# A float64 weight conversion rewritten in 128x512 pieces on VectorE and ScalarE, and the scores and softmax sums of an attention kernel rescheduled

## The chip, the cores and the metric

One core of one Trainium2 chip runs the whole kernel. The metric is device time in microseconds (us) of one execution. Engines are called by the profile's names: PE (TensorE matmul; PEld is its weight load), DVE (VectorE), ACT (ScalarE), POOL (GpSimd) and SP (SyncE, which here only issues DMAs).

## The reference

Attention over 8 batches, 8 heads, 576 positions and a head size of 64, with a threshold under the softmax, feeds a two-layer network with a quick GELU. The two weight matrices arrive as float64, everything else as float32.

```python
scores = scale * np.matmul(q, k.transpose(0, 1, 3, 2))
thresh = np.max(scores, axis=-1, keepdims=True) - tau
scores = np.where(scores >= thresh, scores, -1000000000.0)
scores = scores - np.max(scores, axis=-1, keepdims=True)
attn = np.exp(scores)
attn = attn / (np.sum(attn, axis=-1, keepdims=True) + 1e-09)
out = np.matmul(attn, v)
...
h = x @ w_in                       # x: 4608 x 512, w_in: 512 x 2048
g = h * (1.0 / (1.0 + np.exp(-1.702 * h)))
return (g @ w_out).astype(np.float32)   # w_out: 2048 x 512
```

## The kernel before, in words

**Attention.** The 64 heads are taken as 32 pairs, four to a batch. For a pair, DVE transposes q and k in 32x32 blocks (`prep`, L282), and PE makes the scores with the keys on the partitions: four main tiles of 128 keys and one tail tile that holds the last 64 keys of both heads. `scores` (L291 to L310) makes four matmuls for a main tile (two heads by two halves of the queries) into two PSUM tiles of the pool `psA`, which has three; each `ps` tile is copied to SBUF by ACT (`keep`, L328, 128x576). DVE takes maxima over groups of 32 keys (`in_groups`, L342), finishes them in a few small steps (`over_tiles`, `over_groups`, `lower`: L348 to L371), spreads the thresholds over the keys (`spread_max`, L376) and subtracts them (`sub`, L384 and L387). ACT drives what lies below the threshold far down (`mask`, a Prelu of a steep slope, L393) and takes the exponential (`exps`, L397). PE multiplies by the values (`values`, tile `pv`, L411). The sums of the exponentials come from PE for pairs 0 to 7 (`sums_by_pe`, tile `den`, also L411: matmuls with ones) and from pair 8 on from DVE (`in_groups` once more, with add; the constant is `BY_PE`). DVE turns the sums round and scales the result into the network's input `xT` (`spread_sums`, `place_x`: L459 to L478).

**The network.** The 4608 rows are nine blocks of 512. For each block PE makes 16 groups of four matmuls (`mm1`, tile `hps`, L490), ACT a tanh (L498), DVE the product `gT` (L501), and then PE four groups of 16 matmuls (`mm2`, tile `ops`, L509). One program matmul of float32 shows as two records in the trace. Block 0 needs pairs 0 to 3; block 1 holds rows of batches 0 and 1, so its first matmul needs `xT` of pairs 4 to 7.

**The weights.** `pieces` are 64 parts of 128x256: first w_in, then w_out. Each is loaded twice, once as it lies (`w64`) and once shifted by three bytes (`w64s`), so that exponent and 28 bits of mantissa can be cut out as 32-bit integers. `cv_open` on DVE makes mantissa `frac` (L239, L243) and exponent `ex` (L248); `cv_mant` on ACT (L256) makes the mantissa a float; `cv_exp` and `cv_end` on POOL (L262, L265, L272) clamp and shift the exponent and multiply. Three pieces can be in load and two in conversion.

**The order.** A planner at the end of the kernel writes each engine's instructions in a fixed order: every step is a `task` with an engine, an assumed cost, a rank, the tasks it follows, and the buffers it takes and gives (`limits`). `run_in_order` plays these through and, on each free engine, starts the ready task of lowest rank. mm1 and mm2 have the highest rank number, so PE takes them only where no attention step is ready. On the chip each engine then works through its list in order and waits at semaphores. While block 0 has not begun, the pairs 1 and 3 use the space of `gT` for their buffers (`APART`).

Of the kernel before, what the change touches and what calls it, by code (L numbers as in the profile page):

```python
# [10 lines left out]
FP32 = mybir.dt.float32  # L11
# [8 lines left out]
P = 128  # L20
GELU_SCALE = 1.702
EPS = 1e-9
BIG = 3.0e38
# [7 lines left out]
def kernel(  # L31
# [62 lines left out]
    neg = const.tile([P, 1], FP32, name="neg")  # L94
    scl = const.tile([P, 1], FP32, name="scl")
    gap = const.tile([P, 1], FP32, name="gap")
# [8 lines left out]
              "raw0": 1, "raw1": 1, "qkT0": 1, "qkT1": 1, "v_m": 2, "w64": 3, "cv": 2}  # L105
# [57 lines left out]


# [44 lines left out]
    WC = 256  # L209
    wide = moe_w_in.dtype != FP32  # L210
    pieces = [(w_in, moe_w_in, c, j) for j in range(d_ff // WC) for c in range(NDC)]
    pieces += [(w_out, moe_w_out, c, j) for c in range(NFC) for j in range(d_model // WC)]
    cv = {}

    def load_w(i):
# [7 lines left out]
        t = work.tile([P, WC, 2], U32, name="w64", tag="w64", bufs=3)  # L223
        nc.sync.dma_start(out=t.rearrange("p c w -> p (c w)"), in_=dram.bitcast(U32))
        t3 = work.tile([P, WC, 2], U32, name="w64s", tag="w64s", bufs=3)
# [4 lines left out]
        cv[i] = [t, t3]  # L230


    def cv_open(i):
        t, t3 = cv[i]
        hi = t[:, :, 1]


        frac = work.tile([P, WC], I32, name="frac", tag="frac")
        nc.vector.tensor_scalar(  # L239
            out=frac, in0=t3[:, :, 0].bitcast(I32), scalar1=0x0FFFFFFF, scalar2=0x10000000,  # L240
            op0=ALU.bitwise_and, op1=ALU.bitwise_or,
        )
        nc.vector.scalar_tensor_tensor(  # L243
            out=frac, in0=hi.bitcast(I32), scalar=31, in1=frac,
            op0=ALU.arith_shift_right, op1=ALU.bitwise_xor,
        )
        ex = work.tile([P, WC], U32, name="ex", tag="ex")
        nc.vector.tensor_scalar(  # L248
            out=ex, in0=hi, scalar1=20, scalar2=0x7FF,
            op0=ALU.logical_shift_right, op1=ALU.bitwise_and,  # L250
        )
        cv[i] = [frac, ex]

    def cv_mant(i):
        mant = work.tile([P, WC], FP32, name="mant", tag="mant")
        nc.scalar.activation(out=mant, in_=cv[i][0], func=AF.Copy, scale=2.0**-28)  # L256
        cv[i][0] = mant

    def cv_exp(i):

        ex = cv[i][1]
        nc.gpsimd.tensor_scalar(  # L262
            out=ex, in0=ex, scalar1=1150.0, scalar2=896.0, op0=ALU.min, op1=ALU.max
        )
        nc.gpsimd.tensor_scalar(  # L265
            out=ex, in0=ex, scalar1=-896.0, scalar2=2.0**23, op0=ALU.add, op1=ALU.mult
        )

    def cv_end(i):
        dst, _, c, j = pieces[i]  # L270
        mant, ex = cv.pop(i)
        nc.gpsimd.tensor_tensor(  # L272
            out=dst[:, c, ts(j, WC)], in0=mant, in1=ex.bitcast(FP32), op=ALU.mult
        )
# [19 lines left out]
    def scores(n, t):  # L294
        qT, kT = mats[n, 0], mats[n, 1]
        if t == NKT:
            ps = [psA.tile([P, 2, 512], FP32, name="ps", tag="ps")]
            for c in range(2):
                nc.tensor.matmul(  # L299
                    ps[0][:, c, 0:SH], lhsT=kd[n % 2], rhs=qT[:, ts(c, SH)],  # L300
# [3 lines left out]
        else:  # L304
            ps = [psA.tile([P, 2, 512], FP32, name="ps", tag="ps") for _ in range(2)]
            for c in range(2):
                for h in range(2):
                    nc.tensor.matmul(  # L308
                        ps[h][:, c, 0:SH],
                        lhsT=kT[ts(h, D), ts(t, P)], rhs=qT[ts(h, D), ts(c, SH)],  # L310
                        start=True, stop=True,
                    )
        pss[n, t] = ps

    def keep(n, t, h):
        ps = pss[n, t][h]
        if t == NKT:
            st = work.tile([P, S], FP32, name="s_t", tag="s_t", bufs=2)
            o = st
        else:  # L320
            if h == 0:
# [400 lines left out]
```

## Time and profile before

| what | value |
|---|---|
| median of three timed runs (lowest, highest) | 1480.32 us (1479.87, 1480.63) |
| the profiled execution: time, span in the profile | 1479.97 us, 1478.2 us |
| PE, DVE, ACT, POOL busy | 1417.4, 988.5, 662.2, 113.2 us |
| PE's instructions: `ops` and `hps` (network) | 1152 + 1152 records |

In the profile, a row of a timeline has start, length (both us), engine, line, operation, tiles, shape and count, and in brackets the idle time before it with what ended it. "busy" counts overlapping instructions of an engine once; the mean of a group counts each instruction in full. The chain of waits lists pieces of the chain that ended last as start, length, what, and a record count that holds matmuls and weight loads or halves of matmuls as they came.

### The profile page before, as it was taken

Reading aid. Unit: us, or ns where it says so; the run is one execution under the profiler, and the core shown is the slowest. Engines: PE = TensorE matmul, PEld = TensorE weight load, DVE = VectorE, ACT = ScalarE, POOL = GpSimd, SP = SyncE. Lnnn points to the kernel's source line nnn. Section 1 sums busy time; section 2 is a strip of 40 time slices with the busy share of each in tenths; the row PEclk is TensorE's granted clock in tenths of the full one; section 3 lists DMA queues with packets and bytes.
Section 4 is the critical chain, followed back from the end, with each engine's and each line's share of the span. In section 5 each row is a group of like instructions: output and inputs, shape, how many; then the busy total and the mean of one; then the engine's idle time right before and its main releaser. Section 6 shows DMA issues by size and latency. Waiting matters only on the chain.

```text
span 1478.2 us, 14382 instructions
## 1 busy us (share of the span) xinstructions
PE 1417.4 (96%) x5056; PEld 661.5 (45%) x5056; DVE 988.5 (67%) x1678; ACT 662.2 (45%) x917; POOL 113.2 (8%) x204
## 2 busy tenths in 40 slices
PE   6888948999999999999999999999999999999998
PEld 3443414444444444444444444444444444444443
DVE  7989898448888888878788887888767840200200
ACT  6774443445544554555455555565444530100100
POOL 0127675000000000000000000000000000000000
PEclk9999979999999999999999999999999999999999
DMA  7236865210111111111111111111111000000000
GB/s 132 67 91 211 236 216 159 40 38 18 25 36 43 32 25 32 39 32 24 25 39 39 24 24 32 39 32 24 32 39 24 1 8 22 0 7 22 0 7 22
DMA packets 214296, 72.23 MB, mean 49 GB/s; under 512 B 193232, under 2 KB 201424, under 8 KB 214224
## 3 DMA queue, kind: packets, MB, share of 16 engines
q1 hardware_dynamic: 211856, 71.02, 19.7%
q8 instruction: 40, 0.66, 0.2%
q10 hardware_dynamic: 2368, 0.30, 0.2%
q14 instruction: 32, 0.26, 0.1%
HBM read 61.84 MB, written 9.44 MB: 48 GB/s over the span
## 4 chain that ended last, share of the span: by engine, by line
PE 82%; DVE 11%; DMA 2%; issue 2%; ACT 2%; SPq 0%; DVEq 0%; ACTq 0%
PE ops L509 31%; PE hps L490 30%; PE pv L411 9%; PE ps L308 8%; PE ps L299 2%; DVE frac L239 1%; DVE ex L248 1%; PE den L411 1%; DVE part L342 1%; DMA w64s<-in_moe_w_out_dram 1%; DVE s_m L384 1%; DVE frac L243 1%; DVE gT L501 1%; DVE s_t L387 0%; DVE qkT L282 0%
## 5 line engine op out<-in xcount | busy, mean ns | idle before, releaser
L509 PE MATMUL ops<-w_out,gT 128*128 128x512 f32 x1152 | 513.8, 600 | 22.4 <-POOL w_out L272 21.3
L490 PE MATMUL hps<-xT,w_in 128*128 128x512 f32 x1152 | 509.6, 596 | 4.9 <-DVE gT L501 4.2
L342 DVE TRANSPOSE_TENSOR_REDUCE part<-s_m 128x36 f32<-128x1152 f32 x216 | 290.3, 1361 | 111.7 <-ACT s_m L328 107.2
L509 PEld LDWEIGHTS ops<-w_out,gT 128*128 128x128 f32 x1152 | 215.8, 191 | 294.4 <-issue 259.5
L490 PEld LDWEIGHTS hps<-xT,w_in 128*128 128x128 f32 x1152 | 215.0, 190 | 273.8 <-issue 249.2
L328 ACT COPY s_m<-ps 128x576 f32<-128x576 f32 x240 | 142.0, 641 | 251.6 <-PE ps L308 251.4
L501 DVE SCALAR_TENSOR_TENSOR gT<-th,hps 128x512 f32<-128x512 f32 x144 | 96.7, 672 | 213.4 <-ACT th L498 212.8
L393 ACT ACTIVATE s_m<-s_m 128x1152 f32<-128x1152 f32 x120 | 138.3, 1153 | 71.6 <-DVE s_m L384 71.5
L498 ACT ACTIVATE th<-hps 128x512 f32<-128x512 f32 x144 | 84.9, 590 | 185.1 <-PE hps L490 185.1
L308 PE MATMUL ps<-qkT 64*128 64x288 f32 x960 | 154.3, 436 | 12.5 <-DVE qkT L282 10.0
L397 ACT ACTIVATE s_m<-s_m,shift,scl 128x1152 f32<-128x1152 f32 x120 | 161.3, 1344 | 2.8
L384 DVE TENSOR_TENSOR s_m<-s_m,mb 128x1152 f32<-128x1152 f32 x120 | 156.7, 1352 | 0.8
L308 PEld LDWEIGHTS ps<-qkT 64*128 64x128 f32 x960 | 86.5, 189 | 106.2 <-ACT s_m L328 37.7
L411 PE MATMUL pv<-s_m,v_m 128*64 128x288 f32 x960 | 125.7, 414 | 0.0
L516 ACT ACTIVATE osb<-ops 128x512 f32<-128x512 f32 x36 | 21.3, 592 | 211.4 <-PE ops L509 211.4
L411 PEld LDWEIGHTS pv<-s_m,v_m 128*64 128x64 f32 x960 | 67.7, 139 | 61.6 <-issue 7.6
L256 ACT ACTIVATE mant<-frac 128x256 f32<-128x256 int32 x64 | 26.2, 415 | 55.2 <-DVE frac L243 55.0
L282 DVE STREAM_TRANSPOSE qkT<-q_raw 128x576 f32<-128x576 f32 x30 | 23.3, 776 | 40.1 <-PE ps L299 36.7
L387 DVE TENSOR_TENSOR s_t<-s_t,mb 64x576 f32<-64x576 f32 x60 | 45.1, 752 | 0.4
L342 DVE TRANSPOSE_TENSOR_REDUCE part_t<-s_t 128x18 f32<-128x576 f32 x56 | 41.8, 747 | 1.4 <-ACT s_t L397 0.4
L376 DVE STREAM_TRANSPOSE mb<-thr 128x1152 f32<-128x1152 f32 x30 | 41.3, 1377 | 0.9
L262 POOL TENSOR_SCALAR ex<-ex 128x256 uint32<-128x256 uint32 x64 | 30.6, 477 | 120.9 <-DVE ex L248 119.4
(64 smaller groups left out, 754.1 us busy)
## 6 DMA issues: line engine op xcount, KB each, us to landing
out_dram<-osb SPq DMA_DIRECT2D x36, 256.0 KB, 2.0
q_raw<-in_q_dram SPq DMA_DIRECT2D x120, 72.0 KB, 2.4
k_raw<-in_k_dram SPq DMA_DIRECT2D x116, 72.0 KB, 2.4
v_m<-in_v_dram SPq DMA_DIRECT2D x64, 128.0 KB, 2.4
w<-in_moe_w_in_dram SPq DMA_DIRECT2D x32, 256.0 KB, 3.1
w<-in_moe_w_out_dram SPq DMA_DIRECT2D x32, 256.0 KB, 3.4
w64s<-in_moe_w_in_dram SPq DMA_DIRECT2D x32, 255.6 KB, 3.4
w64s<-in_moe_w_out_dram SPq DMA_DIRECT2D x32, 255.6 KB, 3.7
```

The source lines that it names most:

```text
L308: nc.tensor.matmul(ps[h][:, c, 0:SH], lhsT=kT[ts(h, D), ts(t, P)], rhs=qT[ts(h, D), ts(c, SH)], start=True, stop=True,)
L328: nc.scalar.copy(out=halves(o), in_=ps[:, :, 0:SH])
L342: nc.vector.tensor_reduce(out=o, in_=i, axis=AXL.X, op=op, apply_transpose=True)
L384: nc.vector.tensor_tensor(out=s, in0=s, in1=mb, op=ALU.subtract)
L387: nc.vector.tensor_tensor(out=s[ts(h, D)], in0=s[ts(h, D)], in1=mb[ts(h, D), h, :], op=ALU.subtract)
L393: nc.scalar.activation(out=s, in_=s, func=AF.Prelu, alpha=STEEP)
L397: nc.scalar.activation(out=s, in_=s, func=AF.Exp, scale=scl, bias=shift)
L411: nc.tensor.matmul(o[c][ts(h, D), 0:SH], lhsT=lhsT, rhs=rhs, start=(t == 0), stop=(t == NKT),)
L490: nc.tensor.matmul(hidden[j], lhsT=w_in[:, c, ts(j, P)], rhs=xTs[blk][:, c, :], start=(c == 0), stop=(c == NDC - 1),)
L498: nc.scalar.activation(out=ths[j], in_=hidden[j], func=AF.Tanh, scale=GELU_SCALE / 2)
L501: nc.vector.scalar_tensor_tensor(out=gT[j], in0=ths.pop(j), scalar=1.0, in1=hidden.pop(j), op0=ALU.add, op1=ALU.mult)
L509: nc.tensor.matmul(acc[i], lhsT=gT[j][:, ts(i, P)], rhs=w_out[:, j, :], start=(j == 0), stop=(j == NFC - 1),)
```

## The change

It does six things.

- Weight pieces are 128x512 (32 instead of 64). All steps work in place, in the loaded words. DVE cuts out the exponent (`cv_ex`, L258 of the changed kernel), ACT turns it into a power of two with one Relu (`cv_power`, L266), DVE cuts out the mantissa (`cv_frac`, L272 and L276), and one DVE instruction converts, scales and multiplies (`cv_end`, L284). POOL has no part any more, and there is no clamp from above.
- Loads land in one of two `w64`/`w64s` buffer pairs or in one of four parts of `w_out` itself (`stage`), of four rows each. A piece of `w_out` may be written only when the stage that lies over it is through.
- The ranks move: w_in pieces have ranks from 3.6 to 4.1, w_out pieces from 3.84 to 4.74 (before: 3.2 to 4.2 for both).
- `scores` makes one `ps` tile from two matmuls, one for each head, for one half of the queries; it is a task of its own, so a main tile has two such tasks, each with one `ps` buffer and one `keep`.
- `BY_PE` is 5: sums of pairs 5, 6 and 7 come from DVE.
- The scale of the scores moves from the exponential to the subtraction, which becomes a scalar_tensor_tensor (L394, L400); the exponential keeps only the pointer `shift`.

```diff
-    WC = 256
+    WC = 512
...
+    STAGES = 4
+    PER_STAGE = NFC // STAGES
+
+    def stage(i):
+
+        if i < n_in:
+            return i % (STAGES + 2) if i % (STAGES + 2) < STAGES else None
+        i -= n_in
+        return STAGES - 1 if i % 3 == 0 and i < NFC - PER_STAGE else None
...
+        x = stage(i)
+        if x is None:
+            t = work.tile([P, WC, 2], U32, name="w64", tag="w64", bufs=2)
+            t3 = work.tile([P, WC, 2], U32, name="w64s", tag="w64s", bufs=2)
+        else:
+            rows = [w_out[:, ds(PER_STAGE * x + 2 * y, 2), :] for y in range(2)]
...
+    def cv_ex(i):
+        hi, ex, _ = cv[i]
         nc.vector.tensor_scalar(
             out=ex, in0=hi, scalar1=20, scalar2=0x7FF,
             op0=ALU.logical_shift_right, op1=ALU.bitwise_and,
         )
...
+    def cv_power(i):
+
+        ex = cv[i][1].bitcast(I32)
+        nc.scalar.activation(out=ex, in_=ex, func=AF.Relu, scale=2.0**23, bias=rebias)
...
+    def cv_frac(i):
+
+
+        hi, _, frac = cv[i]
+        nc.vector.tensor_scalar(
+            out=frac.bitcast(I32), in0=frac.bitcast(I32), scalar1=0x0FFFFFFF,
+            scalar2=0x10000000, op0=ALU.bitwise_and, op1=ALU.bitwise_or,
+        )
+        nc.vector.scalar_tensor_tensor(
+            out=frac.bitcast(I32), in0=hi.bitcast(I32), scalar=31, in1=frac.bitcast(I32),
+            op0=ALU.arith_shift_right, op1=ALU.bitwise_xor,
         )
 
     def cv_end(i):
         dst, _, c, j = pieces[i]
-        mant, ex = cv.pop(i)
-        nc.gpsimd.tensor_tensor(
-            out=dst[:, c, ts(j, WC)], in0=mant, in1=ex.bitcast(FP32), op=ALU.mult
+        _, power, frac = cv.pop(i)
+        nc.vector.scalar_tensor_tensor(
+            out=dst[:, c, ts(j, WC)], in0=frac.bitcast(I32), scalar=2.0**-28,
+            in1=power.bitcast(FP32), op0=ALU.mult, op1=ALU.mult,
         )
...
+        ps = psA.tile([P, 2, 512], FP32, name="ps", tag="ps")
...
+            for h in range(2):
+                nc.tensor.matmul(
+                    ps[:, h, 0:SH],
+                    lhsT=kT[ts(h, D), ts(t, P)], rhs=qT[ts(h, D), ts(c, SH)],
+                    start=True, stop=True,
+                )
...
-            nc.vector.tensor_tensor(out=s, in0=s, in1=mb, op=ALU.subtract)
+            nc.vector.scalar_tensor_tensor(
+                out=s, in0=s, scalar=scl, in1=mb, op0=ALU.mult, op1=ALU.subtract
+            )
...
-        nc.scalar.activation(out=s, in_=s, func=AF.Exp, scale=scl, bias=shift)
+        nc.scalar.activation(out=s, in_=s, func=AF.Exp, bias=shift)
...
-    BY_PE = 8
+    BY_PE = 5
...
-        a = task("SP", 1.1, rank, load_w, i, take=("w64",), lag=3.5)
-        a = task("DVE", 1.0, rank, cv_open, i, after=[a], take=("cv",), give=("w64",))
-        m = task("ACT", 0.42, rank, cv_mant, i, after=[a])
-        e = task("POOL", 1.0, rank, cv_exp, i, after=[a])
-        ready_w.append(task("POOL", 0.9, rank, cv_end, i, after=[e, m], give=("cv",)))
+        x = stage(i)
+        place = ("w64",) if x is None else (f"stage{x}",)
+        a = task("SP", 1.1, rank, load_w, i, take=place, lag=5.0)
+        e = task("DVE", 0.44, rank, cv_ex, i, after=[a])
+        m = task("ACT", 0.72, rank, cv_power, i, after=[e])
+        a = task("DVE", 1.14, rank, cv_frac, i, after=[e])
+
+        over = [ready_w[y] for y in range(i) if i >= n_in and stage(y) == (i - n_in) // PER_STAGE]
+        ready_w.append(task("DVE", 0.72, rank, cv_end, i, after=[a, m] + over, give=place))
```

On DVE, this is what stands before, in the middle of block 0's first half (`gT<-th,hps` is the network's product, `frac`, `ex` and `w` the conversion, a number behind a name its buffer):

```order
L501 SCALAR_TENSOR_TENSOR gT<-th,hps 128x512
L239 TENSOR_SCALAR frac<-w64s 128x256
L243 SCALAR_TENSOR_TENSOR frac<-w_944,frac 128x256
L248 TENSOR_SCALAR ex<-w_944 128x256
L348 TENSOR_REDUCE red<-part 128x36
```

And this is what stands there now, a little later in the program, among the pieces of w_out:

```order
L272 TENSOR_SCALAR w64s<-w64s 128x512
L276 SCALAR_TENSOR_TENSOR w64s<-w_1236,w64s 128x512
L515 SCALAR_TENSOR_TENSOR gT<-th,hps 128x512
L284 SCALAR_TENSOR_TENSOR w_out<-w64s,w_1236 128x512
L258 TENSOR_SCALAR w_1253<-w_1253 128x512
```

A piece costs DVE four instructions of twice the length instead of three, for twice the elements; the product into `w_out` has come over from POOL. Up to the last step of pair 3 on DVE, 8 pieces of 256 were opened before; now 10 pieces of 512 are opened and 7 of them finished. The last `cv_end` now stands inside pair 5's subtractions; before, the last `cv_open` stood behind pair 5's `place_x`.

On PE, before, a late pair's scores stand in four groups with two network matmuls between them (`pv` the values of the pair before, `ps` scores, `kd` the tail tile):

```order
L411 MATMUL pv<-s_t,v_t_74 64x288 x4
L308 MATMUL ps<-qkT 128x288 x4
L490 MATMUL hps<-xT,w_in 128x512 x2
L308 MATMUL ps<-qkT 128x288 x4
L490 MATMUL hps<-xT,w_in 128x512 x2
L308 MATMUL ps<-qkT 128x288 x4
L490 MATMUL hps<-xT,w_in 128x512 x2
L308 MATMUL ps<-qkT 128x288 x4
L299 MATMUL ps<-qkT,kd_73 128x288 x2
L490 MATMUL hps<-xT,w_in 128x512 x24
```

Now the same place reads:

```order
L425 MATMUL pv<-s_t,v_t_74 64x288 x4
L504 MATMUL hps<-xT,w_in 128x512 x6
L319 MATMUL ps<-qkT 128x288 x16
L312 MATMUL ps<-qkT,kd_73 128x288 x2
L504 MATMUL hps<-xT,w_in 128x512 x26
```

From pair 9 on, 12 pairs have three groups (4, 4, and 8 with the tail), pair 13 has four, pair 22 two, and the last nine pairs one.

On PE, before, around the values of pair 7, the last pair that block 1 needs (`ops` the output matmuls of block 0, `den` the sums):

```order
L509 MATMUL ops<-w_out,gT 128x512 x6
L411 MATMUL pv<-s_m,v_m 64x288 x16
L411 MATMUL pv<-s_t,v_t_75 64x288 x4
L411 MATMUL den<-s_m,ones 64x288 x16
L411 MATMUL den<-s_t,ones_t 64x288 x4
L509 MATMUL ops<-w_out,gT 128x512 x2
```

And now:

```order
L523 MATMUL ops<-w_out,gT 128x512 x10
L319 MATMUL ps<-qkT 128x288 x4
L425 MATMUL pv<-s_m,v_m 64x288 x16
L425 MATMUL pv<-s_t,v_t_75 64x288 x4
L319 MATMUL ps<-qkT 128x288 x12
L312 MATMUL ps<-qkT,kd_72 128x288 x2
L504 MATMUL hps<-xT,w_in 128x512 x28
```

The sums (`den`) of pairs 5 to 7 are gone from PE. Between pair 7's scores and pair 7's values stand now 10 network matmuls and 4 of pair 8's scores.

116 lines of the change are left out of this document (40 added, 76 removed).

## The prediction

> **What bounds the kernel now.** I read the span and its slices first, then the stages.
>
> ```profile
> span 1478.2 us, 14382 instructions
> PE   6888948999999999999999999999999999999998
> DVE  7989898448888888878788887888767840200200
> ```
>
> PE is full from the eighth slice to the end; only the first seven hold idle PE, and there DVE is the full engine. So the time is where the dense part begins, plus PE's work behind that. I cut at three events: pair 3 placed (111.6 us), the last weight conversion opened on DVE (249.2), block 1's first matmul (324.7).
>
> ```profile
> core 0: us, PE busy (x) PEld busy (x) DVE busy (x) ACT busy (x) POOL busy (x), PEclk, DMA share, GB/s
> 0.00:111.60 111.60, 84.13 (x496) 46.13 (x496) 94.85 (x163) 76.35 (x103) 13.86 (x36) 0.91 0.44 98
> 111.60:249.20 137.60, 111.30 (x394) 49.62 (x394) 124.71 (x251) 63.49 (x115) 97.77 (x165) 0.90 0.72 217
> 249.20:324.70 75.50, 72.86 (x319) 34.96 (x319) 39.46 (x64) 33.16 (x42) 1.53 (x3) 1.00 0.16 35
> 324.70:1478.20 1153.50, 1149.08 (x3850) 530.78 (x3848) 729.43 (x1204) 489.23 (x658) 0.00 (x0) 1.00 0.12 25
> ...
> 251.07 11.43 PE L509 MATMUL ops<-w_out,gT 128*128 128x512 f32 x26 [2.89 <-POOL w_out L272]
> ...
> 324.68 1.98 PE L490 MATMUL hps<-xT,w_in 128*128 128x512 f32 x4
> ```
>
> DVE has 16.8 us idle in the first stage and 12.9 in the second; PE's last wait for w_out ends at 251.07. In the last stage PE idles 4.4 of 1153.5 us. In the third, DVE is half idle.
>
> **The second stage: conversion.**
>
> ```profile
> L243 DVE SCALAR_TENSOR_TENSOR frac<-w,frac 128x256 int32<-128x256 int32 x56 | 30.5, 545 | 1.9
> L248 DVE TENSOR_SCALAR ex<-w 128x256 uint32<-128x256 uint32 x56 | 25.8, 461 | 0.0
> L239 DVE TENSOR_SCALAR frac<-w64s 128x256 int32<-128x256 int32 x56 | 23.8, 425 | 9.0 <-DMA w64s<-in_moe_w_out_dram 6.1 <-DMA w64s<-in_moe_w_in_dram 2.7
> ...
> 111.53 0.28 DVE L239 TENSOR_SCALAR frac<-w64s 128x256 int32<-128x256 int32 x1
> 111.84 0.43 DVE L243 SCALAR_TENSOR_TENSOR frac<-w,frac 128x256 int32<-128x256 int32 x1
> 112.19 0.29 DVE L248 TENSOR_SCALAR ex<-w 128x256 uint32<-128x256 uint32 x1
> ...
> 122.40 0.81 DVE L248 TENSOR_SCALAR ex<-w 128x256 uint32<-128x256 uint32 x1
> ...
> 122.28 0.78 POOL L272 TENSOR_TENSOR w_in<-mant,ex 128x256 f32<-128x256 f32 x1
> ```
>
> With POOL idle (111.5) the three take 0.28, 0.43 and 0.29 us; their means are 0.42, 0.55 and 0.46. The 0.81 us one began 0.12 behind POOL's product and ended 0.15 behind it (123.21 against 123.06). So much of the cost is waiting for POOL, and POOL has nothing left to do in the change. The Trainium skill (SBUF — State Buffer, "Who interferes with whom") says that VectorE and GpSimd share one port pair as an exclusive lock, so the later of the two blocks. By that rule the waits go entirely and the 0.81 us row agrees with it; if the excess came from the strided words instead, the sum would be the second rival's.
>
> For 512 elements I have no row; rows of other lengths bound each kind; the reduction stands here for later.
>
> ```profile
> L371 DVE COPY thr<-thr 32x36 f32<-32x36 f32 x32 | 5.5, 172 | 1.1
> L384 DVE TENSOR_TENSOR s_m<-s_m,mb 128x1152 f32<-128x1152 f32 x120 | 156.7, 1352 | 0.8
> L342 DVE TRANSPOSE_TENSOR_REDUCE part<-s_m 128x36 f32<-128x1152 f32 x216 | 290.3, 1361 | 111.7 <-ACT s_m L328 107.2
> 24.61 5.16 DVE L384 TENSOR_TENSOR s_m<-s_m,mb 128x1152 f32<-128x1152 f32 x4
> ```
>
> One input: from 36 elements (0.172) to 256 (0.285) the slope is 0.51 ns, so 512 take 0.42 us. Two inputs: from 256 (0.43) to 1152 (1.352) it is 1.03 ns, so 0.69. Instructions in a row overlap by 0.06 us (four of 1.352 fill 5.16). A piece of 512 thus costs DVE 2 x 0.42 + 2 x 0.69 - 4 x 0.06 = 1.98 us. Before, two of 256 cost 2 x (30.5 + 25.8 + 23.8) / 56 = 2.86.
>
> First stage: DVE opens 10 pieces of 512 and finishes 7: 37 instructions, 20.1 us less 2.2 of overlap. Gone from it are 8 pieces of 256 (11.4), two reductions of pair 4 (2.7) and its two transposes of 576 (1.5, as one of 1152 below takes 1.38). Net +2, so pair 3 is placed at 113.6, provided that six loads of twice 512 KB land in time. They stand on SP behind pair 2's q and k; pair 3's q and k queue behind them, but are wanted only after 70 us.
>
> Second stage: 91 conversion instructions (44 x 0.42 + 47 x 0.69 = 50.9, less 5.5: 45.4). The rest was 124.7 - 80.1 = 44.6 by the rows above, or about 49 with overlaps given back, and loses about 6: a reduction and a subtraction (2.7 by their rows), two half-length tail subtractions (1.4) and the short instructions of one placing (an estimate of 2). I take 43. With the old idle of 12.9 that makes 101, so the last conversion ends at 214.6, against 251.0 now. PE needs 64 `hps` matmuls (54.9), two pairs' scores (about 13) and pair 4's values and sums (9.9) by then: 78, which hides. ACT's conversion (32 instead of 64 instructions) fits into its idle half.
>
> **From there to block 1.** PE has 50 matmuls of block 0 left, and pairs 5, 6 and 7 must pass one after the other.
>
> ```profile
> 1156.79 5.00 PE pv L411 x40
> 1161.79 1.17 PE ps L308 x8
> 1162.96 1.91 PE hps L490 x4
> 1164.88 1.17 PE ps L308 x8
> ...
> 1254.12 54.93 PE hps L490 x128
> ...
> 313.73 4.85 PE den L411 x40
> ...
> 20.87 0.36 DVE L348 TENSOR_REDUCE red<-part 128x36 f32<-128x144 f32 x1
> ...
> 23.20 1.38 DVE L376 STREAM_TRANSPOSE mb<-thr 128x1152 f32<-128x1152 f32 x1
> ...
> 26.07 1.16 ACT L393 ACTIVATE s_m<-s_m 128x1152 f32<-128x1152 f32 x1 [1.33 <-DVE s_m L384]
> 28.52 1.15 ACT L393 ACTIVATE s_m<-s_m 128x1152 f32<-128x1152 f32 x1
> ```
>
> A network matmul costs 54.93 / 64 = 0.858 us, a pair's values 5.0. A four-matmul group of scores takes 1.17 and makes the two network matmuls behind it cost 1.91 instead of 1.72. After the last conversion: 10 matmuls (8.6), values of pair 5 (5.0), scores of pair 6 in three groups (2 x 3.08 + 3.1): 22.9. Then copy (0.6), tail reduction (0.75), small steps (2.3), spread (1.4), first subtraction (1.3), four mask-and-exponential pairs of 2.45 and a tail of 1.5: 17.7, at 40.6; PE meanwhile has 22 matmuls (18.9), till 41.8. Values of pair 6 to 46.8, scores of pair 7 to 56.1, their exponentials at 73.8: here PE has only 10 matmuls and four scores (9.8) and waits 7.9. Values to 78.8, rest of pair 8's scores (4.4): block 1 at +83.2. DVE's part is 21 reductions, 9 + 6 subtractions and small steps, 67 us in all, and stays beside it; taking 4.85 us of sums from PE three times gains nothing here beyond what this chain leaves.
>
> A wait of 8 us also costs clock:
>
> ```profile
> 200.00:210.00 10.00, 2.72 (x4) 0.50 (x2) 9.83 (x17) 5.04 (x7) 7.44 (x10) 0.58 0.65 214
> ...
> 224.45 2.29 PE L308 MATMUL ps<-qkT 64*128 64x288 f32 x8
> 226.67 5.13 PE L411 MATMUL pv<-s_m,v_m 128*64 128x288 f32 x32
> ...
> 239.47 1.24 PE L308 MATMUL ps<-qkT 64*128 64x288 f32 x8
> ```
>
> With PE mostly idle its granted clock was 0.58, and the first group of scores took 2.29 instead of 1.24 us, the values behind it 5.13 for 32 records (4.0 at 5.00 for 40): 2.1 more. I add 2. The Trainium skill (TensorE: Matmul & The Clock Gate, "What's actually happening") halves the clock after one idle window of about 3.4 us and restores it after one busy window; by that the loss is at most about 1.7 us, and nothing if the wait stays short. Block 1 begins at 214.6 + 85.2 = 300 (now 324.7).
>
> **The dense rest.** Before, 1153.5: 1024 matmuls 879, values of 24 pairs 120, and 154 for scores of pairs 9 to 31 with the last of pair 8's. That last piece (2.4) is now ahead of block 1. A group of scores costs 1.17 - 8 x 4.85 / 40 = 0.20 on entry and 0.19 on exit: 0.39. 12 pairs lose one group, one two, nine three: 41 groups, 16.0 us. But in one run of nine units ACT's copies pace PE:
>
> ```profile
> L328 ACT COPY s_m<-ps 128x576 f32<-128x576 f32 x240 | 142.0, 641 | 251.6 <-PE ps L308 251.4
> 21.80 1.29 PE L308 MATMUL ps<-gT 64*128 64x288 f32 x8 [0.20 <-ACT gT L328]
> ```
>
> Two matmuls take 0.485 us, a copy 0.64; with three buffers six units wait 0.156 each, 0.94 a run, 8.4 in nine runs (nil if copies overlap, 2.3 a run at the 1.49 us per two copies of this row). Net gain 7.6; the rest is 1153.5 - 2.4 - 7.6 = 1143.5. The exponential without its scale pointer, the subtraction with one, the constants and the planner's 1.79 change nothing that I can price above 1 us: DVE and ACT have slack there.
>
> **Sum.** Span 300 + 1143.5 = 1443.5; the execution took 1.8 more than its span, so 1445, against 1479.97 (median of the runs 1480.32). I say **1445**, 2.4% faster.
>
> **Rivals.**
>
> *Slots pace w_out.* Ten of the last loads share two `w64` pairs.
>
> ```profile
> w<-in_moe_w_out_dram SPq DMA_DIRECT2D x32, 256.0 KB, 3.4
> w64s<-in_moe_w_out_dram SPq DMA_DIRECT2D x32, 255.6 KB, 3.7
> ```
>
> Twice the size lands in 3.7 to 7.4 us; with issue, four conversion steps and ACT a slot turns in 8.5 to 13. Five turns are 43 to 65 us, against some 51 of DVE time from the first of them to the end. The upper end adds 14: **1459**. Each next load also waits in SP's queue ahead of q, k and v loads. Chance 0.13.
>
> *DVE stays slow.* If the means of 0.44 and 0.55 scale, not 0.285 and 0.43, a piece costs 2 x 0.22 + 2 x 0.19 = 0.82 more, 32 of them 26: **1471**. The undisturbed rows speak against it. Chance 0.09.
>
> *The long run blocks PE: slower.* PE takes its list in order. If ACT is inside a mask-and-exponential pair when the third unit of a run wants its buffer, PE waits up to 2.45 us; over 23 pairs 56: **1501**. It decides from (1480 - 1445) / 23 = 1.5 us a pair. Against it: values stand ahead of the scores, and they already waited for those exponentials. Chance 0.03.
>
> *The gain does not come.* PE is 96% busy, and if block 1 still began near 325 (pairs 5 to 7 paced by DVE, which now makes four more reductions of 1.36 us and a tail for each) only the scores' gain were left: **1470**. Chance 0.05, as DVE is half idle there.
>
> **Chances and range.** The forecast has 0.70, with 1425 to 1459 as its own range: downwards the second stage's idle (10), the copies' waits (8) and the clock (2); upwards the 14 above. Taking in the slow DVE: 1425 to 1471. Faster by over 0.2% (about what a measurement of this kernel can tell from no change) 0.95, within 0.02, slower 0.03.
>
> **What would show it.** Right: `frac` and `ex` of 512 at 0.42 and 0.69 us; pair 3 placed near 114, last `cv_end` near 215, block 1 near 300; a PE wait ahead of pair 7's values; later runs of 16 scores with ACT as releaser. Wrong: PE waits for `w_out` past 230, DVE idle for `w64s` loads, or over 1.5 us of waits in each run of scores.

## The result, and the profile after

The changed kernel takes **1447.47 us** (median of 4 runs, 1446.35 to 1448.91) against 1480.39 for the kernel before (4 runs): ratio 0.9779, 95% interval 0.9762 to 0.9796. The profiled execution took 1448.37 with a span of 1446.5.

The changed kernel's page: the span, each engine's busy time, and the slices.

```profile
span 1446.5 us, 13628 instructions
PE 1384.0 (96%) x4936; PEld 650.1 (45%) x4936; DVE 997.7 (69%) x1650; ACT 643.6 (44%) x885; POOL 1.3 (0%) x13
PE   5769979899999999999999999999999999999998
DVE  7998998888978888888878886788777820200100
```

PE's busy time fell from 1417.4 to 1384.0 us, by 33.4; its idle time went from 60.8 (1478.2 - 1417.4) to 62.5. So the 31.7 us by which the span fell are work that PE lost, and its idle time as a whole did not shrink. That is not how the prediction told it, and the experiments are about this.

The changed kernel cut at the same three events (pair 3 placed, last conversion, block 1), and one stretch of the kernel before, from the end of PE's last wait for `w_out` to block 1. Columns: span of the window, then the busy time of PE, PEld, DVE, ACT and POOL, PE's granted clock, DMA.

```profile
0.00:117.40 117.40, 76.93 (x469) 41.92 (x470) 101.43 (x169) 73.76 (x95) 1.34 (x13) 0.84 0.53 152
117.40:216.40 99.00, 90.12 (x308) 40.58 (x306) 91.79 (x162) 50.50 (x74) 0.00 (x0) 0.97 0.68 222
216.40:304.85 88.45, 79.06 (x326) 38.83 (x327) 72.54 (x119) 46.73 (x63) 0.00 (x0) 0.92 0.20 43
304.85:1446.50 1141.65, 1137.85 (x3837) 528.83 (x3835) 731.89 (x1204) 472.65 (x654) 0.00 (x0) 1.00 0.12 25
```

```profile
251.07:324.68 73.61, 72.84 (x319) 34.93 (x319) 37.59 (x62) 32.83 (x41) 0.00 (x0) 1.00 0.17 36
```

PE's idle time has moved. Ahead of the last conversion it went from 55.6 us (251.07 less the 84.13 and 111.31 us of work) to 49.4, behind it from 0.8 to 9.4, and in the last stage from 4.4 to 3.8.

The conversion ends 34.7 us earlier (216.4 against 251.07). Behind it the kernel before had 72.8 us of PE work and 0.8 of waiting; the changed one has 79.1 and 9.4. So 14.8 of the 34.7 is given back. The last stage is 11.9 shorter.

The changed kernel's conversion by groups (count, busy time, mean ns of one, idle ahead). L258 extracts the exponent, L272 and L276 build the fraction, L284 is the product.

```profile
L258 DVE TENSOR_SCALAR w<-w 128x512 uint32<-128x512 uint32 x16 | 6.8, 423 | 0.0
L272 DVE TENSOR_SCALAR w64s<-w64s 128x512 int32<-128x512 int32 x16 | 6.8, 425 | 2.2 <-DMA w64s<-in_moe_w_out_dram 1.6 <-DMA w64s<-in_moe_w_in_dram 0.6
L276 DVE SCALAR_TENSOR_TENSOR w64s<-w,w64s 128x512 int32<-128x512 int32 x16 | 11.1, 694 | 0.5
L284 DVE SCALAR_TENSOR_TENSOR w_out<-w64s,w 128x512 f32<-128x512 int32 x12 | 8.2, 684 | 0.5
```

These are the interpolated values to 0.01 (0.42 and 0.69), and loads keep VectorE waiting for 2.2 us in this group.

The changed kernel's PE in order of time from the last wait for `w_out` to block 1 (start, duration, name, records; in brackets the wait ahead and what ended it).

```profile
216.36 10.30 PE L523 MATMUL ops<-w_out,gT 128*128 128x512 f32 x18 [6.28 <-DVE w_out L284]
226.59 4.10 PE L425 MATMUL pv<-s_m,v_m 128*64 128x288 f32 x32
...
259.99 4.10 PE L425 MATMUL pv<-s_m,v_m 128*64 128x288 f32 x32
...
274.42 8.75 PE L523 MATMUL ops<-w_out,gT 128*128 128x512 f32 x20
292.55 2.29 PE L319 MATMUL ps<-qkT 64*128 64x288 f32 x8 [9.39 <-DVE qkT L295]
294.77 4.75 PE L425 MATMUL pv<-s_m,v_m 128*64 128x288 f32 x32
...
300.42 3.42 PE L319 MATMUL ps<-qkT 64*128 64x288 f32 x24
303.78 1.24 PE L312 MATMUL ps<-qkT,kd 128*128 128x288 f32 x4
304.85 1.45 PE L504 MATMUL hps<-xT,w_in 128*128 128x512 f32 x3
```

From 216.36 to 283.2 PE is full. Then it stands 9.39 us ahead of four scores of pair 8; pair 7's values follow. VectorE makes pair 8's transposes only behind pair 7's subtractions and three of pair 7's sum reductions, which stood on PE before:

```profile
285.52 1.64 DVE L400 SCALAR_TENSOR_TENSOR s_t<-s_t,scl,mb 64x576 f32<-64x576 f32 x2
287.19 3.90 DVE L352 TRANSPOSE_TENSOR_REDUCE part<-s_m 128x36 f32<-128x1152 f32 x3
291.01 0.73 DVE L295 STREAM_TRANSPOSE qkT<-q_raw 128x576 f32<-128x576 f32 x1
```

A late pair of the changed kernel, on PE and on ACT.

```profile
977.97 4.42 PE L319 MATMUL ps<-qkT 64*128 64x288 f32 x32
982.32 1.24 PE L312 MATMUL ps<-qkT,kd 128*128 128x288 f32 x4
983.39 17.18 PE L504 MATMUL hps<-xT,w_in 128*128 128x512 f32 x39
```

```profile
978.77 4.44 ACT L338 COPY s_m<-ps 128x576 f32<-128x576 f32 x8 [1.82 <-PE ps L319]
```

Sixteen scores take 4.35 us start to start (977.97 to 982.32) against 16 x 0.2425 = 3.88 at the pace of the prediction's row of the sums (two records of its 4.85 us for 40). Of the 0.47 more, 0.20 is the cost of a group on entry, which the prediction counts by itself; about 0.27 is left. The copies, 4.44 / 8 = 0.555 each in a row against 0.485 for the two matmuls that fill a buffer, thus pace PE a little: an estimate of 0.27 us a run.

### The profile page after: what moved, and what is told of

The parts are those of the page before. It is cut to its first block, busy times and chain, and to the rows that moved or that the text cites. A ratio compares the mean times of both kernels' runs of the same rounds, so it can differ in the third digit from the quotient of the medians.

```text
span 1446.5 us, 13628 instructions
## 1 busy us (share of the span) xinstructions
PE 1384.0 (96%) x4936; PEld 650.1 (45%) x4936; DVE 997.7 (69%) x1650; ACT 643.6 (44%) x885; POOL 1.3 (0%) x13
## 4 chain that ended last, share of the span: by engine, by line
PE 88%; DVE 8%; ACT 1%; DMA 1%; issue 1%; DVEq 0%; ACTq 0%; SPq 0%
PE ops L523 33%; PE hps L504 31%; PE pv L425 11%; PE ps L319 9%; PE ps L312 2%; PE den L425 2%; DVE part L352 1%; DVE s_m L394 1%; DMA w64s<-in_moe_w_out_dram 1%; DVE mb L386 1%; DVE gT L515 0%; DVE w_out L284 0%; DVE w64s L276 0%; DVE part_t L352 0%; ACT s_m L338 0%
## 5 line engine op out<-in xcount | busy, mean ns | idle before, releaser
L523 PE MATMUL ops<-w_out,gT 128*128 128x512 f32 x1152 | 507.0, 597 | 7.4 <-DVE w_out L284 7.3
L352 DVE TRANSPOSE_TENSOR_REDUCE part<-s_m 128x36 f32<-128x1152 f32 x228 | 301.3, 1355 | 107.4 <-ACT s_m L338 106.5
L338 ACT COPY s_m<-ps 128x576 f32<-128x576 f32 x240 | 137.2, 657 | 144.5 <-PE ps L319 143.3
L394 DVE SCALAR_TENSOR_TENSOR s_m<-s_m,scl,mb 128x1152 f32<-128x1152 f32 x120 | 163.3, 1411 | 0.6
L319 PE MATMUL ps<-qkT 64*128 64x288 f32 x960 | 141.8, 433 | 17.3 <-DVE qkT L295 17.3
L411 ACT ACTIVATE s_m<-s_m,shift 128x1152 f32<-128x1152 f32 x120 | 150.2, 1252 | 2.5
L400 DVE SCALAR_TENSOR_TENSOR s_t<-s_t,scl,mb 64x576 f32<-64x576 f32 x60 | 48.7, 812 | 0.4
L492 DVE TENSOR_TENSOR xT<-pv,rc 128x288 f32<-128x288 f32 (+8 forms) x96 | 28.4, 351 | 22.4 <-PE pv L425 21.1
L312 PE MATMUL ps<-qkT,kd 128*128 128x288 f32 x120 | 37.1, 432 | 0.0
L425 PE MATMUL pv<-s_t,v_t 128*64 128x288 f32 x256 | 36.5, 406 | 0.0
```

Source lines behind the costliest of these rows:

```text
L312: nc.tensor.matmul(ps[:, i, 0:SH], lhsT=kd[n % 2], rhs=qT[:, ts(i, SH)], start=True, stop=True,)
L319: nc.tensor.matmul(ps[:, h, 0:SH], lhsT=kT[ts(h, D), ts(t, P)], rhs=qT[ts(h, D), ts(c, SH)], start=True, stop=True,)
L338: nc.scalar.copy(out=o, in_=pss.pop((n, t, c))[:, :, 0:SH])
L352: nc.vector.tensor_reduce(out=o, in_=i, axis=AXL.X, op=op, apply_transpose=True)
L394: nc.vector.scalar_tensor_tensor(out=s, in0=s, scalar=scl, in1=mb, op0=ALU.mult, op1=ALU.subtract)
L411: nc.scalar.activation(out=s, in_=s, func=AF.Exp, bias=shift)
```

## The experiments

**Theory after the result.** Up to block 1 two engines are nearly full, one behind the other: VectorE up to the last conversion, PE behind it. A part that frees one of them is worth its time only where the other has room. **Rival**: the parts are worth what each takes off one path, and add up; the conversion then brings some 25 us and the scores 10, as the prediction's sum has it, the sums nothing.

### One part alone, one part undone

*The conversion alone* (the kernel before with the new conversion):

```
-    WC = 256
+    WC = 512
...
+    STAGES = 4
+    PER_STAGE = NFC // STAGES
...
+        m = task("ACT", 0.72, rank, cv_power, i, after=[e])
+        a = task("DVE", 1.14, rank, cv_frac, i, after=[e])
...
     BY_PE = 8
```

> The kernel before with the new weight conversion alone: scores in groups of four matmuls and the sums of pairs 5 to 7 on PE stay as before. My theory (the conversion bounds the start, the rest is a small gain of its own): the last conversion ends near 216, as with the whole change (216.3), block 1's first matmul at 302 to 310, and behind it the 1153.5 us of the kernel before; in all 1457 to 1465, about 0.987 of the time before, some two thirds of the whole change's 32.9 us. Rival (the gain is mainly the PE work that the other two parts remove): at most 10 us, 1470 or more.

Measured: 1476.81, ratio 0.9975 (0.9966 to 0.9985), 3.6 us. My number (two thirds of the gain) was far off and the rival's is right, though its reason, that PE's removed work is the gain by itself, falls with the next run. Its windows:

```profile
0.00:107.60 107.60, 76.16 (x465) 42.46 (x465) 92.14 (x156) 73.59 (x92) 1.33 (x13) 0.90 0.52 131
107.60:220.50 112.90, 96.65 (x312) 42.54 (x310) 97.02 (x176) 51.81 (x76) 0.00 (x0) 0.95 0.68 228
220.50:322.80 102.30, 92.88 (x427) 45.37 (x427) 49.72 (x76) 46.34 (x59) 0.00 (x0) 0.92 0.18 37
```

The conversion does end at 220.5, and yet block 1 begins at 322.8. PE still has 92.9 us of work behind it, where the kernel before had 72.8, and waits another 9.4, of which 8.8 stand ahead of four scores and pair 7's values. Ahead of it PE idles 31.4 + 16.3 = 47.7; the kernel before idled 55.6 there. So 30 us of earlier weights buy 8 us of idle time, and the chain of the pairs takes those back.

*The two other parts alone* (the changed kernel with the old conversion):

```
-    WC = 512
+    WC = 256
...
-        ready_w.append(task("DVE", 0.72, rank, cv_end, i, after=[a, m] + over, give=place))
+        ready_w.append(task("POOL", 0.9, rank, cv_end, i, after=[e, m], give=("cv",)))
...
     BY_PE = 5
```

> The changed kernel with the old weight conversion (256 pieces, products on POOL); scores in runs and sums of pairs 5 to 7 on VectorE stay changed. My theory: the last wait for w_out still ends near 250, block 1 begins at 318 to 325, and behind it come 1142 us instead of 1153.5; in all 1463 to 1470, a gain of 10 to 17. Rival (PE's removed work is the gain): the three sums of 4.85 and the 11.9 us of scores both count, 1454 or less.

Measured: 1474.04, ratio 0.9956 (0.9941 to 0.9971), 6.4 us: below my range of gains, and further still from the rival's. PE's work falls to 1390.1 us, but its idle time rises from 60.8 to 81.5 (of a span of 1471.6): the conversion ends at 264.1, 13 us later than before.

*The sums back on PE*: in the changed kernel `BY_PE = 5` becomes `BY_PE = 8`.

> The changed kernel with the sums of pairs 5 to 7 back on TensorE, 3 x 4.85 = 14.5 us more for it and about 19 us of reductions less for VectorE. My theory (behind the last conversion the chain through the three pairs sets block 1, with 9.4 us of PE waiting there): most of it goes into waits, 1446 to 1453. Rival (PE is the bound there, so each sum counts): 1459 to 1462.

Measured: 1460.63, ratio 0.9863 (0.9846 to 0.9879): 13.2 us more than the changed kernel. The rival holds; each sum costs 4.4 of its 4.85 us. Behind the last conversion PE has 15.8 us more work (94.8 against 79.1) and only 3.0 less waiting (6.4 instead of 9.4). The sums of pairs 5 and 6 stand between a pair's values and the next pair's later scores, so they delay the start of the very chain for which PE waits at its end, and the wait can't absorb them. It shrinks a little because pair 8's transposes then stand directly behind pair 7's subtractions, with no sum reductions between.

*The sums alone* (the kernel before with `BY_PE = 5`):

> The kernel before with one number altered: the sums of pairs 5 to 7 on VectorE, the old conversion and the old scores. My theory (what a part gains depends on which engine the others leave full: with the old conversion VectorE's extra 6 us for pair 5 stand ahead of the last conversion): the last conversion ends 5 to 15 us later than 251, PE's work behind it is 10 to 15 shorter, and the time is 1475 to 1482. Rival (a sum taken from PE is worth its 4.4 us in any setting): 1465 to 1469.

Measured: 1474.90, ratio 0.9966 (0.9952 to 0.998), 6.2 us, 0.1 below my range. The same edit is worth half of what it is in the changed kernel, so the rival fails here; but my mechanism fails too, since the conversion ended at 248.6 and not later than 251. What rose is PE's waiting (1472.3 - 1402.0 = 70.3 against 60.8), 14.4 us of it for transposes of q and k (10.0 before).

*The scores in groups again* (the changed kernel with four matmuls over two buffers):

```
-                    "PE", 1.1 if tail else 0.58, r, scores, n, t, c,
+                "PE", 1.1 if tail else 1.2, r, scores, n, t,
...
-                    take=("psA", "s_t") if tail else ("psA",) + (own(n, "s_m") if c == 0 else ()),
+                take=("psA", "s_t") if tail else ("psA", "psA") + own(n, "s_m"),
```

> The changed kernel with the scores in groups of four matmuls over two buffers again. My theory (each switch of matmul kind costs PE about 0.2 us, so fewer groups gain what the trace shows behind block 1): the stretch from block 1's first matmul to the end goes back from 1141.7 to 1150 to 1154, block 1 begins within 3 us of 304.9; in all 1454 to 1462. Rival (ACT's copies eat in the long runs what the fewer switches gain): 1445 to 1450.

Measured: 1462.30, ratio 0.9876 (0.9861 to 0.9891), 14.8 us more. The theory holds, though the time and the last stage (1154.5) lie just past my ranges. From its windows, the first and the last:

```profile
0.00:105.70 105.70, 74.65 (x464) 43.20 (x464) 92.97 (x151) 71.88 (x92) 1.33 (x13) 0.90 0.50 132
...
306.40:1460.90 1154.50, 1150.26 (x3849) 530.31 (x3848) 737.07 (x1205) 479.33 (x658) 0.00 (x0) 1.00 0.12 25
```

The last stage is 12.9 longer, and the first (up to the first `hps` matmul) 9.8 shorter than the changed kernel's 115.5. The long runs thus delay the first four pairs, which costs little in the end: the last conversion stands at 215.0 here and at 216.3 there.

Together, by medians against the runs of the kernel before in the same series ("last conversion" is the end of the last instruction that writes `w_out`):

| conversion | scores | sums | last conversion | block 1 | gain, us |
|---|---|---|---|---|---|
| old | old | VectorE | 248.6 | 319.0 | 6.2 |
| old | new | VectorE | 264.1 | 330.4 | 6.4 |
| new | old | PE | 220.5 | 322.8 | 3.6 |
| new | new | PE | 217.8 | 319.0 | 19.8 |
| new | old | VectorE | 215.0 | 306.4 | 18.1 |
| new | new | VectorE | 216.3 | 304.9 | 32.9 |

Undone one by one, the parts are worth 26.5 (conversion), 14.8 (scores) and 13.1 (sums), 54.4 in all, against 32.9 for the whole. The gains do not add: the conversion is worth 3.6 while PE keeps its work and 26.5 once that is gone, and the scores 0.2 with the old conversion (6.4 - 6.2) and 14.8 with the new. Once the conversion is new, scores and sums do nearly add: on top of its 3.6 the scores bring 16.2 (19.8 - 3.6), the sums 14.5 (18.1 - 3.6), and both 29.3. So the conversion decides how much work taken from PE is worth.

Two things are not separated. The scores alone (old conversion, sums on PE) were not run. And the scale's move to the subtraction is in every row here but those of the conversion alone and the sums alone, so differences with these two hold it as well.

### What the conversion's speed rests on

*POOL at work again* (the changed kernel; the scratch tile is read by nobody):

```
+    def on_pool(i):
+        dst, _, c, j = pieces[i]
+        x = dst[:, c, ds(j * WC, 256)]
+        for _ in range(4):
+            nc.gpsimd.tensor_tensor(out=idle, in0=x, in1=x, op=ALU.mult)
...
+        task("POOL", 3.2, rank, on_pool, i, after=ready_w[-1:])
```

> The changed kernel with POOL at work again: behind each finished piece POOL multiplies 256 of its columns four times into a scratch tile that nobody reads, about 100 us of POOL in all, as in the kernel before; the output doesn't change. My theory (VectorE's old means were waits for POOL): the one-input steps of 512 rise from 0.42 to 0.5 us or more and the two-input ones from 0.69 to 0.78 or more, with single ones over 1 us, the last conversion ends 10 to 25 us later than 216, and the time is 1455 to 1470. Rival (POOL and VectorE do not hinder each other; the old cost came from the strided words or the size): 0.42 and 0.69 stay, 1446 to 1449.

Measured: 1468.63, ratio 0.9921 (0.9906 to 0.9936); the last conversion ends at 237.1, 20.8 later, and the time is 21.2 longer. Its groups on VectorE between 120 and 230 us:

```profile
L277 DVE SCALAR_TENSOR_TENSOR w64s<-w,w64s 128x512 int32<-128x512 int32 x13 | 12.2, 937 | 0.4
L358 DVE TRANSPOSE_TENSOR_REDUCE part<-s_m 128x36 f32<-128x1152 f32 x8 | 10.9, 1365 | 0.0
L273 DVE TENSOR_SCALAR w64s<-w64s 128x512 int32<-128x512 int32 x13 | 9.6, 740 | 0.0
```

The same instructions on the same data take 0.94 instead of 0.69 and 0.74 instead of 0.43 us beside a busy POOL; the reduction keeps its 1.36. So a busy POOL raises the means by a third to seven tenths; before they stood a quarter to six tenths above the undisturbed values. The Trainium skill (SBUF — State Buffer, "Who interferes with whom") says that a reduction never contends with GpSimd, while `tensor_scalar` in a two-port mode does, and an instruction with two inputs in SBUF does against a GpSimd instruction that reads SBUF: these rows agree, though none shows in which mode `tensor_scalar` ran.

*Pieces of 256 on VectorE and ACT* (the changed kernel with `WC = 256`, four half-size `w64` pairs, no staging):

> The changed kernel with pieces of 256 columns in four pairs of w64 buffers of half the size (the same memory), none staged. My theory (what counts is VectorE's time: 2 x 0.285 + 2 x 0.43 - 0.24 = 1.19 us a piece, 64 of them 76 us against 63): the last conversion ends near 229, in all 1453 to 1462. Rival (the size of a piece is what freed VectorE from the 545 and 461 ns means): the four instructions keep those means, the conversion ends past 250, 1470 or more.

Measured: 1464.21, ratio 0.9891 (0.9876 to 0.9906), slightly past my range. The group that stands for the rest:

```profile
L273 DVE SCALAR_TENSOR_TENSOR w64s<-w,w64s 128x256 int32<-128x256 int32 x64 | 27.4, 428 | 2.2
```

That is the undisturbed 0.43 and not the 0.545 of the kernel before, so the rival is out, and the old means were waits for POOL: strided words of this size cost 0.43 with POOL idle. The size by itself only saves the fixed part of an instruction (0.69 for 512 against twice 0.43). The last conversion ends at 236.4, 20 later. VectorE's busy time rises by 12.2 us (1009.9 - 997.7), as estimated; up to the last conversion it is 15.6 us more (208.75 against 193.13), since some other work now stands ahead of it, and 4.5 us of idle time come on top. That part I did not foresee, and as this run also takes the staging away, it need not come from the size.

*No staging* (the changed kernel; `stage` gives none, so all 32 pieces share two `w64` pairs):

```
     def stage(i):
-        if i < n_in:
-            return i % (STAGES + 2) if i % (STAGES + 2) < STAGES else None
-        i -= n_in
-        return STAGES - 1 if i % 3 == 0 and i < NFC - PER_STAGE else None
+        return None
```

> The changed kernel with all 32 weight pieces in the two w64 pairs, none staged in w_out. My theory (VectorE is never short of pieces only because six places are in turn): with two places a turn of 8.5 to 13 us, 16 turns need 136 to 208 us, so the last conversion ends past 235, VectorE waits for loads over 20 us in all, and the time is 1458 to 1475. Rival (two places of 512 feed VectorE well enough): 1446 to 1450.

Measured: 1460.37, ratio 0.9858 (0.9841 to 0.9875); the last conversion ends at 251.9. Two places are too few, and PE now waits for `w_in`. My 20 us of VectorE waiting for loads did not show (5.2 us in its first fraction step): the planner knows of the two places and writes late pieces late into VectorE's list. Up to the last conversion VectorE has 23.7 us more work (216.87 against 193.13) and 11.9 more idle time. PE's two longest waits for `w_in`:

```profile
189.97 2.07 PE L501 MATMUL hps<-xT,w_in 128*128 128x512 f32 x2 [8.20 <-DVE w_in L281]
199.29 9.12 PE L501 MATMUL hps<-xT,w_in 128*128 128x512 f32 x14 [7.25 <-DVE w_in L281]
```

Of 35.6 us on the conversion 12.9 reach the end, while of POOL's 20.8 all did. Here PE does more of its work ahead of the last conversion (850 records against 774); beside the busy POOL it did not (774 as well), so all the work behind it was still to do.

### The two waits behind the conversion

*Transposes one pair early* (the changed kernel, all pairs):

```
-        pq = task("DVE", 0.78, r, prep, n, 0, ...
-        pk = task("DVE", 0.78, r, prep, n, 1, ...
+        pq = task("DVE", 0.78, r - 1.0, prep, n, 0, ...
+        pk = task("DVE", 0.78, r - 1.0, prep, n, 1, ...
```

> The changed kernel with one rank altered: VectorE transposes a pair's q and k one pair earlier, so that the scores of pair 4 stand ahead of pair 3's values on PE and the transposes of pair 8 ahead of pair 7's subtractions. My theory (the 9.39 us in which PE waits for the transposes of pair 8 are on the path): that wait falls under 4 us, block 1 begins at 297 to 302, in all 1440 to 1445. Rival (pair 7's values are not to be had earlier, so another wait takes its place): 1446 to 1449.

Measured: 1450.30, ratio 0.9798 (0.9784 to 0.9813), no gain (2.8 us more than the changed kernel), and the wait is still there:

```profile
293.61 2.29 PE L319 MATMUL ps<-qkT 64*128 64x288 f32 x8 [11.11 <-DVE qkT L295]
```

A rank of 8 - 1 only ties with pair 7's work, and ties go to the earlier task, so pair 8's transposes stayed where they were. The run moved other scores (pair 4's) instead and says nothing about the wait; the next does.

*Pair 8's transposes ahead of pair 7's work*: `r - 1.5 if n == 2 * NPAIR else r` in the same two tasks.

> The changed kernel with the two transposes of pair 8 ranked ahead of pair 7's work on VectorE, and nothing else. My theory (the wait of 9.39 us is for those transposes, since PE's list has four scores of pair 8 ahead of pair 7's values): PE does twelve of pair 8's scores while it waits for pair 7's exponentials, the wait shrinks to 3 to 6 us ahead of pair 7's values, block 1 begins near 300 and the time is 1441 to 1445. Rival (those 1.4 us on VectorE and the copies on ACT push pair 7's exponentials back by as much): 1446 to 1449.

Measured: 1444.02, ratio 0.9747 (0.9733 to 0.9762). PE around the place:

```profile
277.53 3.33 PE L319 MATMUL ps<-qkT 64*128 64x288 f32 x24
280.79 5.42 PE L523 MATMUL ops<-w_out,gT 128*128 128x512 f32 x12
286.14 2.51 PE L425 MATMUL pv<-s_m,v_m 128*64 128x288 f32 x16
290.28 1.19 PE L425 MATMUL pv<-s_m,v_m 128*64 128x288 f32 x8 [1.63 <-ACT s_m L411]
```

The 9.39 us wait is gone, twelve scores stand in its place, and pair 7's values now wait for their exponentials in pieces of 1.63 us and less. Block 1 begins at 297.7 instead of 304.9, but the last stage grows by 3.2 (1144.9), as early network matmuls wait there 1.49 us for pair 7's placing and 1.84 for the network's own product. Of the 9.4 us, 3.5 were to be had (4.2 if each time is held against the kernel before of its own series).

*Block 0's second matmuls in turns* (the changed kernel):

```
-        for i in range(BLK // P):
-            for p in range(NFC // 2):
+        for i, p in turns(blk):
...
+    def turns(blk):
+        if blk:
+            return [(i, p) for i in range(BLK // P) for p in range(NFC // 2)]
+        return [(i, p) for h in (0, 2) for p in range(NFC // 2) for i in (h, h + 1)]
```

> The changed kernel with the second matmuls of block 0 in another order: the first two row groups take turns by pairs of rows of w_out, then the other two, so PE has twice the work for each row that is converted. My theory (the 7.3 us in which PE waits for w_out are lost, since the pairs' chain begins behind them): pair 5's values begin at 219 to 222 instead of 226.6, and the gain of 4 to 7 us reaches the end, 1440 to 1444. Rival (the network matmuls are then missing as cover between pair 6 and pair 7): 1446 to 1449.

Measured: 1442.34, ratio 0.974 (0.9725 to 0.9754), **5.1 us below the changed kernel** (5.9 if each time is held against its own series). From the edit before it differs by less than the runs of the two spread.

```profile
193.98 29.74 PE L523 MATMUL ops<-w_out,gT 128*128 128x512 f32 x68
223.65 4.10 PE L425 MATMUL pv<-s_m,v_m 128*64 128x288 f32 x32
...
281.27 2.19 PE L425 MATMUL pv<-s_m,v_m 128*64 128x288 f32 x8 [9.63 <-ACT s_m L411]
```

With two row groups for each converted row the wait for `w_out` is gone without remainder: 29.74 us in one piece. Pair 5's values come 2.9 us earlier (223.65; I had 219 to 222), pair 7's at 281.27 instead of 294.77, and block 1 at 298.5. A wait of the old size stays: 9.63 us, now for pair 7's exponentials.

*Both edits*:

> Both edits together: the transposes of pair 8 early and block 0's second matmuls in turns. My theory (the two waits lie one behind the other on one path): the gains add, 1435 to 1441. Rival (the chain through pair 7's exponentials takes both in the end): 1440 to 1446.

Measured: 1442.27, ratio 0.9736 (0.9721 to 0.9751), the same as with turns alone. The rival holds: with both edits block 1 begins 4.2 us earlier (294.3), and PE gives that back in two waits behind it (1.99 and 1.84). The versions with turns beat the kernel before and the changed one: their intervals lie wholly below 0.9762, where the changed kernel's begins.

## Why the prediction came out as it did

The time was forecast at 1445 and is 1447.47; the span at 1443.5 and is 1446.5. By its steps:

- **Pair 3 placed**: 113.6 forecast, 117.4 measured. What was left out is that scores in runs delay the first pairs, which the run with scores in groups shows (first network matmul at 105.7 against 115.5). These 9.8 us are more than the 3.8 that the forecast was short, so the rest of this sum stood too high; with the conversion alone the first network matmul came at 107.6, earlier than in the kernel before (112.8), where the forecast had 2 us more.
- **A piece on VectorE**, 0.42 and 0.69 us: measured 0.42 and 0.69. The reason, waiting for POOL, is shown by two runs: POOL back at work costs 20.8 us of conversion, and pieces of 256 without POOL take the undisturbed time.
- **Last conversion**: 214.6 forecast, 216.3 measured. That is nearer than its parts: the first stage took 3.8 longer, the second 2.1 less than the 101 forecast (VectorE's idle time there is 7.2 us and not the old 12.9), and the two cancel in part, which is luck.
- **From there to block 1**: 85.2 forecast, 88.5 measured. A wait near pair 7 came (7.9 forecast, 9.39 measured), but not the one of the prediction. It had PE waiting for pair 7's exponentials; PE waits one place earlier in its list, ahead of pair 8's four scores, for their transposes on VectorE. The prediction has no such step, so that the size came near is luck. In the run with pair 8's transposes ahead, pair 7's values begin at 286.14 instead of 294.77 and do wait for exponentials. The rest of the difference is the clock: I let PE leave the last wait for `w_out` at full speed.

```profile
216.30:219.00 2.70, 2.64 (x3) 1.17 (x4) 2.69 (x4) 2.41 (x4) 0.00 (x0) 0.50 0.00 0
219.00:222.00 3.00, 3.00 (x6) 1.37 (x5) 2.97 (x4) 2.97 (x4) 0.00 (x0) 0.66 0.23 87
222.00:226.50 4.50, 4.50 (x11) 1.71 (x9) 4.50 (x6) 2.01 (x4) 0.00 (x0) 1.00 0.00 0
```

  Behind the 6.28 us wait the granted clock was 0.50 and then 0.66 (the number behind POOL's), which is 2.7 x 0.50 + 3.0 x 0.34 = 2.4 us lost. The loss after the 9.39 us wait was in the forecast, with 2; it was 1.7 (2.29 us instead of 1.24, and 4.75 instead of 4.10). The bound of 1.7 us that the prediction worked out from the Trainium skill (TensorE: Matmul & The Clock Gate, "What's actually happening") fits the second wait and is too low for the first.
- **The last stage**: a gain of 10.0 forecast (2.4 + 7.6), 11.9 measured. Two terms were off and cancel in part. The copies take some 0.27 us a run and not 0.94, since copies in a row overlap; that alone would make it 16.0. But the 0.39 for each of 41 groups counts too much on exit: of the stretches of network matmuls in this stage, 89 before, 62 are left, so only 27 were saved, because many groups stood beside a pair's values. At 0.19 each that takes 2.7 back; the remaining 1.4 stays open. (The prediction's split of the old stage also takes its 4.4 us of idle time into the scores; nothing hangs on that.)
- **The exponentials without their scale pointer and the subtractions with one**: forecast at nothing above 1 us, and not tested by a run. In the last stage that fits, since PE has no wait between 330 and 1440 us. Up to the last conversion, where VectorE is full, 24 subtractions of 0.06 us more are an estimate of 1.4 us.
- **"Taking 4.85 us of sums from PE three times gains nothing here beyond what this chain leaves"**: this step failed. With the sums back on PE the time is 13.2 us longer. The sum of the prediction had come out right because it listed PE's work behind the conversion without the sums, and that list was right; but the sentence takes the wait at the chain's end for room in which the sums could hide, and they stand ahead of it.
- **Where the gain comes from**: the prediction put 24.7 us down to the conversion (block 1 from 324.7 to 300). The number holds only beside the other two parts. Alone the conversion brings 3.6, since PE then has 92.9 us to do behind it. The prediction's own rows have PE busy for 72.86 of the 75.5 us behind the last piece opened, and I should have seen in it that PE is full there: what ends earlier ahead of a full engine is not won.
- **The rivals**: slots did not pace `w_out`, though loads of twice the size landed in 4.8 to 8.5 us instead of the 3.7 to 7.4 assumed; without staging they would have. VectorE did not stay slow. The long run blocked PE by some 0.27 us a pair, far from the 1.5 of that rival. And block 1 did not stay near 325, but with the conversion alone it does (322.8), because of PE's work and not of VectorE's.

In part open is why the last conversion comes at 264.1 with the old conversion, scores in runs and sums on VectorE, against 248.6 with scores in groups. Up to it VectorE has 9.5 us more work there (four more reductions and their small steps, and 3.1 us on subtractions, which carry the scale there and take 1513 ns beside POOL) and 6.0 more idle time, most of it spent waiting for copies of scores. Why the planner's order puts the reductions ahead was not tested.

## What to carry to other kernels

Where two engines are full one behind the other, a part's gain can't be read from that part: cost the change as a whole along both engines, and expect the part that frees the first engine to show little alone. Ask of each wait whether the work that you mean to hide in it stands ahead of its cause; if so, it only moves the wait. When a stage waits for data that arrive row by row, see whether the engine can do more for each row; here that was worth 5 us.

## What the runs showed of the hardware

A short PE wait can cost more than its length. With both last edits PE waited 2.70 us, and the next 24 records of scores took 4.87 us instead of 3.33 (the same 24 in the run with pair 8's transposes alone), at a granted clock of 0.66. It need not: in the run with the sums alone, two network records took 1.13 us behind a wait of 2.87, and 2.08 behind the next, of 3.12. No run here shows a length from which on it does.

```profile
273.99 4.87 PE L319 MATMUL ps<-qkT 64*128 64x288 f32 x24 [2.70 <-DVE qkT L295]
...
234.03 1.13 PE L509 MATMUL ops<-w_out,gT 128*128 128x512 f32 x2 [2.87 <-POOL w_out L272]
238.28 2.08 PE L509 MATMUL ops<-w_out,gT 128*128 128x512 f32 x2 [3.12 <-POOL w_out L272]
```

The exponential of 1152 elements without its scale pointer takes 1252 ns instead of 1344 (first row, the kernel before), and the subtraction with a scale pointer 1411 instead of 1352:

```profile
L397 ACT ACTIVATE s_m<-s_m,shift,scl 128x1152 f32<-128x1152 f32 x120 | 161.3, 1344 | 2.8
...
L411 ACT ACTIVATE s_m<-s_m,shift 128x1152 f32<-128x1152 f32 x120 | 150.2, 1252 | 2.5
L394 DVE SCALAR_TENSOR_TENSOR s_m<-s_m,scl,mb 128x1152 f32<-128x1152 f32 x120 | 163.3, 1411 | 0.6
```
